# A gated dilated convolution: another hand-written order of all instructions, with seven PSUM evictions moved from ScalarE to VectorE

## The chip, the cores and the metric

The kernel runs on one core of a Trainium2 chip. The metric is the device time of one execution in microseconds (us); the median of three executions stands for a kernel. The core has five engines that each work through a list of their own in order: TensorE (PE, the matmuls, with its weight loads as PEld), VectorE (DVE), ScalarE (ACT), GpSimd (POOL) and SyncE (SP, which here only issues DMAs). They wait for each other by semaphores. DMAs are issued from the queues of SP, ACT and POOL.

## The reference

```python
B, T, D, K = (2, 16000, 256, 3)          # x [B,T,D], w [K,D,2D], w_o [D,D], all bfloat16
dil = 2; pad = (K - 1) * dil
xp = jnp.pad(x, ((0, 0), (pad, 0), (0, 0)))
h = jnp.einsum('btc,cd->btd', xp[:, pad:pad + T, :], w[0])
for i in range(1, K):
    off = pad - i * dil
    h = h + jnp.einsum('btc,cd->btd', xp[:, off:off + T, :], w[i])
z = jnp.tanh(h[..., :D]) * jax.nn.sigmoid(h[..., D:])
return z @ w_o
```

Each output row is a three-tap causal convolution over time with a step of two, split into a tanh half and a sigmoid half, multiplied together, and multiplied by a 256x256 matrix.

## The kernel before

The 32,000 rows are cut into 23 groups. Group 0 (kind P, 640 rows) is computed directly with three taps. The others use the fewer products of a polynomial (Toom-Cook) form of the convolution: 18 groups of kind A (1536 rows: 256 columns of 6 neighbouring rows) need five products for three row pairs, 4 groups of kind B (1024 or 640 rows) four products for two row pairs. A group has four **blocks**, one for each 128 of the 512 output channels, so there are 88 blocks; they run in the order 9, 10, 11, 1 to 8, 12 to 22 of the groups. A product is a pair of matmuls over the 256 input channels with 512 moving columns (320 in the last group, 22).

What a block of kind A does, by the letters of the order: `F` first product into PSUM tile `b`; `c` ScalarE copies `b` to `ss` (L390); `M` middle product added to `b`; `h` VectorE makes `hh` from `ss` and `b` (L393), or `k` ScalarE copies `b` to `hh` (L403); `L` last product added to `b`; `A` VectorE makes `a` in PSUM from `ss` and `b`, `Y` VectorE makes `yy` (both L393); `Z` a product added to `b`, which therefore has to wait until `A` and `Y` have read it; `I` a product added to `a`. Then ScalarE applies tanh or sigmoid to `b`, `yy` and `a` (letters `b`, `y`, `a`, L441), and after two blocks VectorE multiplies tanh by sigmoid (`g`, L460, tile `zz`). `P` is an output product (four matmuls of 256 columns, L478, tile `o_ps`), 123 of them besides the last three. Its result is evicted to SBUF by ScalarE (`e`, L495) or by VectorE (`v`, L487), and `s` stores it.

The moving operands (`u0` to `u3`, `e`, `f`, `uh`, `ud` and for kind B `m`, `p`, `d0`, `d3`) are sums and differences of rows, made by VectorE in one piece (L330, scaled copies L328) or by GpSimd in four quarters (a token with `q`, L330). The sums `rm`, `rp`, `r0`, `ri` are made on top of `e`, `f`, `u0`, `u2`: mostly by an adding DMA from GpSimd's queue (a token that ends in `d`, L325). `rm` is used by `M`, `rp` by `L`, `r0` by `Z`, `ri` by `I`. A quarter on GpSimd is held behind a VectorE instruction so many places back (the number after `q`).

The order of everything is one table, `PLAN`: 1730 tokens, read from left to right; each token appends one piece of work to its engine's list. Nothing else orders the work of the main part. PSUM holds three `b` tiles, two `a` tiles and three `o_ps` tiles.

```python
if "q" in token:   on_gpsimd(token)
elif token[-1] == "d":  pre(*group_of(token[:-1]), None)
else:  note(pre(*group_of(token), nc.vector))
...
elif what in "AY":  combine(next(kinds[what]), what.lower())
elif what in "ev":  out_evict(*pieces[int(token[1:])], on_v=what == "v")
```

Of the kernel before, what the change touches and what calls it, by code (L numbers as in the profile page):

```python
# [26 lines left out]
M ud.1 wa.15q28 b I Y k1 F f.1 a Z f.2 c I b L g x M a A F k2 u2.2 P u1.3q14 c L Y e9 M u1.3q54 A y I k3 rp.1d u3.2
P Y a Z L g e10 Z b A f.3q36 P y ud.2 F f.3q28 b Y P c r0.1d rm.1 P y Z ri.1d e.2 e11 F e.3 I b rm.2d M g c F k4 M
u0.2 u0.3q1 a L h5 c I y A f.3q12 L a M f.3q62 Y e12 P A u1.3q8 e13 Z I Y k6 u1.3q43 I b g ri.2d L a rp.2d F u3.3 y
Z A rm.3d c P u1.4 b r0.2d P a Y M rp.3d F y uh.3 Z ud.3 k7 v15 I b L u3.4 e14 ud.4 F f.4q68 c A P c M u0.3q20 Y a M  # L30
e.4 k8 Z k9 g L rm.4d b I u0.3q33 A e17 P a v16 F f.4q36 L y Y s8 P f.4q55 c x A Z y u2.4q74 M Y b I e18 h10 Z a F g
b P c L u2.3 F e19 u1.5 ri.3d M c A I u0.3q60 k11 M Y a L u0.4 y f.4q1 P A k12 I Z e20 r0.3d uh.4 Y P a rp.4d L b
f.5 r0.4d Z y A F b I g c P u2.5q72 y F Y M e21 u3.5 u2.5q4 I c v22 P y u2.4q90 h13 Z a u2.4q16 v23 M b L u2.4q50
h14 a s10 P s9 e24 u2.5q44 A F x y L Y e.5q82 P c A e.5q79 Z e25 Y M e.5q58 y I h15 b e.5q69 Z a g ri.4d F e26 L c I
A f.6q22 b P s11 uh.5 M a u2.5q82 Y F y rp.5d u0.5 P k16 Z e.6 e27 r0.5d L b g I c P u2.6q118 A y F M e28 u1.6q63 Y
P c f.6q1 h17 Z y I ud.5 e29 rm.5 M b s12 L h18 a u2.6q1 x F a P u2.6q45 A c L Y u1.6q20 e30 I A u1.6q108 e31 M Z a
Y u1.6q33 P k19 g ri.5d Z b L e32 u0.6 P f.7q89 y A I b F uh.6 u2.6q46 e33 P Y c F r0.6d u3.6 P y g rm.6d M e34 I
f.6q13 a h20 P c Z y u1.7 L f.6q67 b M A e35 P rp.6d Y F k21 s14 P a e.7 s13 Z c ud.6 I g e36 ri.6d L b M u2.7q71 A
e37 P a h22 F u0.7q137 e38 P Y u0.7q65 c L s15 Z y uh.7 x u2.7q72 A M b I f.7q90 h23 e39 F f.7q1 y Y L c f.7q114 I
v40 a Z u2.7q22 Y a M g P b P k24 A F e41 x L rp.7 e42 P c A Z y u1.8 I u0.8q93 b M Y a P u0.7q161 h25 Z y F uh.8 b  # L40
u3.7 I u2.8 s16 c rm.7d F e43 f.8 M c L g rp.8d k26 M a u2.7q76 A L k27 Y I y u0.8q1 A Z a u0.7q103 P v44 b u0.8q81
L Y y s17 P u0.8q162 A e45 F r0.7d e46 Z ud.7 Y c I ri.7d P b u3.8 r0.8d M u1.9 a Z e.8 k28 F b ud.8 L rm.8d e.9 c I
y g F u2.9q179 M y A P c P e47 h29 f.9q46 M a Y s18 f.9q43 L e48 s1 ri.8 u2.9q60 Z x k30 I A b L u2.9q117 Y a F y
u0.9q14 A Z c I g u0.9q1 b P a M Y F y u0.9q167 h31 I e49 ud.9 Z c u3.9 L b e.10 rm.9d M e50 A P u0.9q89 a F s19 h32
e51 I x Y f.9q75 c P g L a f.9q1 Z e52 Y P b M u0.10q72 A e53 F u1.10 Z c I h33 y P uh.9 b M f.10 s20 r0.9d y L h34
u2.9q136 F e54 A P a L c Y u0.10q111 I y Y u0.10q129 M e55 Z A rp.9d k35 P uh.10 ri.9d b Z g a I L e56 ud.10 u3.10 F
b s21 A P a x F u2.10 c P Y c M y u1.11 Z e57 M h36 b I u3.11 e58 L g u2.11q137 k37 F P a A L y Y u2.11q107 P c A
u2.11q42 Z y I f.11 rm.10d y M Y b u0.10q118 P e59 v60 rp.10d Z k38 s22 F uh.11 r0.10d b g P a L u0.11 c F P e61 A I
e62 ud.11 ri.10q1 M c Y P y r0.11d u1.12 Z y rp.11d M h39 b I e.11 e63 L u3.12 a F ri.10q1 h40 P e64 A P c ri.10q52
L e65 Y u2.11q33 M a s24 g ri.10q10 Z k41 x I b A L a F u2.12q103 Y y I u2.12q220 A c Z uh.12 rm.11d P y Y P b g M y  # L50
s23 F k42 v66 I u1.13q121 c Z v67 a ri.11d L f.12 e68 M b P A s25 e.13q152 P k43 x Y F a e.13q125 L c e.12 u1.13q170
Z e69 A I b M f.13 u1.13q1 e70 P Y a F u2.12q52 P v71 k44 Z c rp.12d g L y rm.12d M b A I k45 ud.12 P u2.13q69 Y a
s26 F e72 u0.12 L u2.13q15 c Z A P y u2.13q63 M Y b I u1.13q210 e73 h46 F a u2.12q15 Z c uh.13 rp.13d I g y L ri.12d
b M ud.13 P A k47 e.14q113 F a Y L c e.13q247 I A y Z e.14q191 e74 M Y e.13q189 P b h48 Z r0.12d y u3.13 F a g L
rm.13d b I f.14 c P u2.14q103 y F A e75 M v76 u0.13q202 I c h49 P u0.13q57 e77 M Y a u2.14q55 s28 L e78 h50 x
# [591 lines left out]
```

## Time and profile before

| | |
|---|---|
| time, median of 3 runs (lowest, highest) | 258.87 us (258.47, 259.78) |
| time of the profiled execution | 258.77 us |
| its span, first to last instruction | 256.6 us |
| GpSimd busy (share of the span) | 176.9 us (69%) |
| adding DMAs from GpSimd's queue: 18 + 16 + 15 + 15, median from issue to landing | 4.6 to 4.8 us |
| evictions on ScalarE / on VectorE (128x512) | 101 / 23 |

The span is what the instructions cover; about 2.2 us of the profiled execution lie around it. An instruction's time in the trace reaches from its start to its last write, and the next one on the engine may start before that: what an engine can do in a stretch is read from one start to the next, not from the durations.

### The profile page before, as it was taken

The page shows a single profiled execution, that of the slowest core. Times are in us where ns is not written, and L with a number is a line of the kernel's source. Part 1 is how long each engine was busy: PE and PEld are TensorE (multiplying, and loading weights), DVE is VectorE, ACT ScalarE, POOL GpSimd, SP SyncE. Part 2 cuts the span into 40 slices and gives each one's busy share as a digit, 9 for nine tenths or more (in the row PEclk, how much of TensorE's full clock was granted, in tenths as well). Part 3 has the DMA queues.
Part 4 walks back from the last instruction along what each step waited for, and adds up shares of the span by engine and source line. Part 5 has one row for each costly group of instructions (what it writes and reads, how often), then busy time and mean ns, then how long its engine had stood idle before and what let it go on. Part 6 is the DMA issues. An engine that isn't in the chain of part 4 may idle for free.

```text
span 256.6 us, 4575 instructions
## 1 busy us (share of the span) xinstructions
PE 249.9 (97%) x1428; PEld 138.0 (54%) x1428; DVE 242.8 (95%) x405; ACT 243.7 (95%) x492; POOL 176.9 (69%) x249
## 2 busy tenths in 40 slices
PE   8999999999999999999999999999999999999992
PEld 4655555555555565545555555555555545555581
DVE  2999999999999999999999999999999999999991
ACT  4988999999999999999999999999999999999893
POOL 1064554997699888499764887999798798897000
PEclk9999999999999999999999999999999999999997
DMA  6999979989989899999999999996999998773054
GB/s 184 213 202 213 196 172 159 232 143 203 187 199 271 187 200 249 182 289 200 200 237 212 249 196 188 290 244 147 212 260 171 216 219 224 198 217 102 0 226 176
DMA packets 84320, 51.73 MB, mean 202 GB/s; under 512 B 69032, under 2 KB 70312, under 8 KB 84296
## 3 DMA queue, kind: packets, MB, share of 16 engines
q1 hardware_dynamic: 74168, 33.71, 54.3%
q0 software_dynamic: 9216, 16.78, 37.7%
q10 hardware_dynamic: 912, 0.95, 1.1%
q8 instruction: 11, 0.18, 0.3%
q14 instruction: 13, 0.11, 0.1%
HBM read 1.25 MB, written 16.38 MB: 69 GB/s over the span
## 4 chain that ended last, share of the span: by engine, by line
PE 82%; DVE 8%; DMA 3%; ACT 2%; issue 2%; ACTq 0%; DVEq 0%
PE b L359 48%; PE o_ps L478 18%; PE a L359 13%; DVE a L393 2%; DMA e<-u 2%; DVE zz L460 2%; DVE yy L393 2%; PE b L379 1%; PE a L379 1%; DMA xn<-in_x_dram 1%; DVE hh L393 1%; ACT osb L495 1%; ACT sg L441 1%; ACT th L441 0%; ACT ss L390 0%
## 5 line engine op out<-in xcount | busy, mean ns | idle before, releaser
L330 POOL TENSOR_TENSOR u<-xt 128x256 bf16<-128x256 bf16 x88 | 66.8, 774 | 15.0 <-PE b L359 8.4
L478 PE MATMUL o_ps<-wo_sb,zz 128*128 128x256 bf16 x496 | 72.0, 273 | 0.0
L495 ACT CAST osb<-o_ps 128x512 bf16<-128x512 f32 x101 | 63.8, 646 | 0.9 <-PE o_ps L478 0.7
L478 PEld LDWEIGHTS <-zz 128*128 128x128 bf16 x496 | 48.5, 98 | 27.6
L393 DVE SCALAR_TENSOR_TENSOR a<-ss,b 128x512 f32<-128x512 f32 (+1 forms) x88 | 59.5, 679 | 2.3 <-PE b L359 1.3
L390 ACT COPY ss<-b 128x512 f32<-128x512 f32 (+1 forms) x88 | 55.0, 628 | 0.9 <-PE b L359 0.6
L359 PEld LDWEIGHTS <-w_sb 128*128 128x128 bf16 x352 | 34.1, 97 | 35.1 <-issue 3.0
L359 PE MATMUL b<-e,wm_sb 128*128 128x512 bf16 x144 | 42.8, 379 | 0.3 <-DMA e<-u 0.3
L359 PE MATMUL b<-u,w_sb 128*128 128x512 bf16 x144 | 42.9, 379 | 0.2
L359 PE MATMUL b<-u,wa_sb 128*128 128x512 bf16 x144 | 42.9, 379 | 0.0
L359 PE MATMUL b<-f,wp_sb 128*128 128x512 bf16 x144 | 42.9, 379 | 0.0
L359 PE MATMUL a<-u,w_sb 128*128 128x512 bf16 x144 | 42.5, 379 | 0.3 <-DVE a L393 0.2
L460 DVE TENSOR_TENSOR zz<-th,sg 128x1536 bf16<-128x1536 bf16 (+2 forms) x46 | 41.3, 897 | 0.2
L441 ACT ACTIVATE th<-b 128x512 bf16<-128x512 f32 (+1 forms) x44 | 28.0, 636 | 1.4 <-ACT ss L390 0.7
L441 ACT ACTIVATE th<-a 128x512 bf16<-128x512 f32 (+1 forms) x44 | 28.6, 649 | 0.3 <-PE a L359 0.2
L441 ACT ACTIVATE sg<-b 128x512 bf16<-128x512 f32 (+1 forms) x44 | 28.0, 635 | 0.6 <-PE b L359 0.5
L441 ACT ACTIVATE sg<-a 128x512 bf16<-128x512 f32 (+1 forms) x44 | 28.3, 642 | 0.0
L359 PEld LDWEIGHTS <-wm_sb 128*128 128x128 bf16 x176 | 17.0, 98 | 17.2 <-DMA e<-u 1.2
L359 PEld LDWEIGHTS <-wp_sb 128*128 128x128 bf16 x176 | 16.9, 98 | 17.3 <-issue 1.6
L393 DVE SCALAR_TENSOR_TENSOR hh<-ss,b 128x512 f32<-128x512 f32 x38 | 25.9, 681 | 0.2
L393 DVE SCALAR_TENSOR_TENSOR yy<-hh,b 128x512 f32<-128x512 f32 x38 | 25.6, 678 | 0.0
L441 ACT ACTIVATE sg<-yy 128x512 bf16<-128x512 f32 x36 | 24.9, 693 | 0.7 <-DVE yy L393 0.7
(68 smaller groups left out, 373.2 us busy)
## 6 DMA issues: line engine op xcount, KB each, us to landing
out_dram<-osb SPq DMA_DIRECT2D x36, 384.0 KB, 3.5
u<-uh POOLq DMA_DIRECT2D x18, 256.0 KB, 4.8
f<-u POOLq DMA_DIRECT2D x16, 256.0 KB, 4.7
u<-ud POOLq DMA_DIRECT2D x15, 256.0 KB, 4.6
e<-u POOLq DMA_DIRECT2D x15, 256.0 KB, 4.8
out_dram<-osb SPq DMA_DIRECT2D x8, 256.0 KB, 3.1
w_sb<-in_w_dram ACTq DMA_DIRECT2D x3, 256.0 KB, 4.1
xt<-in_x_dram SPq DMA_TRANSPOSE x22, 8.0
```

The lines of the kernel that those rows point to most:

```text
L330: ins = eng.tensor_tensor(out=o, in0=a, in1=b, op=op)
L359: nc.tensor.matmul(G[bank, oi][:, :2 * R], lhsT=wmat[:, ct, osl], rhs=G[mv][:, :, ct, :R], start=which == "first" and ct == 0, stop=ct == ...
L379: nc.tensor.matmul(G[bank, oi][:, :4 * r].rearrange("p (j r) -> p j r", j=4), lhsT=w_taps[tap][:, ct, osl], rhs=xt[:, j0:j0 + 4, ct, c0 + ...
L390: nc.scalar.copy(out=G["ss", oi][:, :n], in_=G["b", oi][:, :n])
L393: return note(nc.vector.scalar_tensor_tensor(out=out, in0=in0, scalar=scalar, in1=in1, op0=ALU.mult, op1=op))
L441: nc.scalar.activation(out=G[name, dt][:, j:j + 2, :R], in_=G[bank, oi][:, :2 * R].rearrange("p (q r) -> p q r", q=2), func=(ACT.Tanh, ACT ...
L460: note(nc.vector.tensor_tensor(out=G["z"][:, dt, :, :n], in0=G["th", dt][:, :, :n], in1=G["sg", dt][:, :, :n], op=ALU.mult))
L478: nc.tensor.matmul(o_ps[:, q, :], lhsT=z, rhs=wo_sb[:, dt, :], start=dt == 0 and (q == 0 or len(dts) == NT), stop=dt == NT - 1, skip_group ...
L495: copy(out=G["osb", at][:, 2 * jp:2 * jp + 2, :], in_=o_ps[:])
```

## The change

`PLAN` is replaced by another list; nothing else in the kernel differs. Both have 1730 tokens and the same blocks, products and loads. By kinds the lists differ in these counts: `e` 103 to 96 and `v` 23 to 30 (seven evictions from ScalarE to VectorE); `h` 38 to 37 and `k` 34 to 35; operands made whole on VectorE, without the scaled ones: 74 in both, of other kinds (`u2` 7 to 13, `rp` 2 to 5, `u0` 10 to 11, `r0` 0 to 1, `d3` 2 to 3, against `u1` 15 to 12, `e` 14 to 11, `f` 11 to 8, `rm` 3 to 0); quarters on GpSimd: 176 in both (`u2` 44 to 20 and `ri` 8 to 0, against `e` 16 to 28, `f` 28 to 40, `u1` 12 to 24, and smaller ones); adding DMAs 64 in both (`rp` 16 to 12, `rm` 15 to 18, `ri` 15 to 17, `r0` 18 to 17).

```diff
 PLAN = """
-m.0 d3.0 p.0 F F d0.0 c F c G L w L A c D wa.5q2 D A wa.2q5 Z d0.1 I b D m.1 a L wa.3q1 F d A wa.10q2 Z c p.1 I
+m.0 d0.0 p.0 F F c G D c D d3.0 L w L A D wa.1q4 F A d wa.2q1 Z c d3.1 I b p.1 Z a I G b F m.1 L c d0.1 P wa.0q1 a L
...
```

The first place is on VectorE at half-way: the rows up to the `yy` of block 44 of the 88 (group 8, last block), the last row but one here. In these rows `a`, `hh` and `yy` are the combinations, `zz` a gate product, `ud` and `u` scaled copies, `e` an operand. Before:

```order
L460 TENSOR_TENSOR zz<-th_1701,sg_1720 128x1536
L393 SCALAR_TENSOR_TENSOR yy<-hh,a 128x512
L393 SCALAR_TENSOR_TENSOR hh<-ss,b 128x512
L328 TENSOR_SCALAR ud<-u_1708 128x1024
L328 TENSOR_SCALAR u_1839<-u_1708 128x1024
L330 TENSOR_TENSOR e<-xt 128x1024
L393 SCALAR_TENSOR_TENSOR a<-ss,b 128x512
L393 SCALAR_TENSOR_TENSOR hh<-ss,b 128x512
L393 SCALAR_TENSOR_TENSOR yy<-hh,b 128x512
L460 TENSOR_TENSOR zz<-th_1787,sg_1811 128x1536
```

Now, with the `yy` of block 44 as the last row:

```order
L460 TENSOR_TENSOR zz<-th_1674,sg_1733 128x1536
L393 SCALAR_TENSOR_TENSOR a<-ss,b 128x512
L393 SCALAR_TENSOR_TENSOR yy<-hh,b 128x512
L328 TENSOR_SCALAR u_1833<-u_1672 128x1024
L330 TENSOR_TENSOR e<-xt 128x1024
L460 TENSOR_TENSOR zz<-th_1774,sg_1789 128x1536
L393 SCALAR_TENSOR_TENSOR a<-ss,b 128x512
L328 TENSOR_SCALAR ud<-u_1672 128x1024
L393 SCALAR_TENSOR_TENSOR yy<-hh,a 128x512
```

The gate product that stood behind this `yy` stands ahead of it now. From the start of the list up to this `yy`, VectorE has one `zz`, one operand, one scaled copy and two evictions more, and one `hh` fewer; TensorE has the same 44 blocks' work ahead of the `Z` that waits for it (211 pairs and 53 output products before, 210 and 54 now).

The second place is on GpSimd at about seven eighths of the list: the quarter of `e` and the adding DMA that makes `rm` (`e<-u`) for group 21, the last of kind A. Before:

```order
L330 TENSOR_TENSOR u_3180<-xt 128x256
L330 TENSOR_TENSOR d_3084<-xt 128x160
L330 TENSOR_TENSOR u_3180<-xt 128x256
L330 TENSOR_TENSOR e<-xt 128x256
L325 DMA e<-u_3151 128x1024
L330 TENSOR_TENSOR u_3224<-xt 128x256
L330 TENSOR_TENSOR p<-xt 128x160
```

Now:

```order
L330 TENSOR_TENSOR e<-xt 128x256
L330 TENSOR_TENSOR d_3101<-xt 128x160
L330 TENSOR_TENSOR e<-xt 128x256 x3
L330 TENSOR_TENSOR d_3222<-xt 128x160
L330 TENSOR_TENSOR f<-xt 128x256
L325 DMA e<-u_3254 128x1024
L325 DMA f<-u_2995 128x1024
```

The four quarters of `e` stand closer together, and two adding DMAs follow each other. Between this DMA's token and the `M` that reads its result (group 21, first block) the list has 12 pairs and 5 output products on TensorE before, and 6 pairs and 3 output products now. For the `rm` of group 19 it is the other way: 8 pairs and 2 output products before, 15 and 4 now.

More of the change, by code (lines that the diff above doesn't have):

```diff
@@ L27 @@
[L27 to L31, printed above, removed]
@@ new lines @@
+c ud.6 I f.7 e35 Z u2.7q9 y A M b P u2.7q89 Y P k21 ri.6d e.7 F a g L rm.7d c Z e36 u2.7q123 A P b M Y y I u2.7q34
+h22 e37 F r0.6d Z a g L c I b A P y ud.7 M Y a F e.8q72 e38 h23 I c Z s15 uh.7 L a rp.7 s14 P x b A f.8q95 M y Y
+e.8q143 F k24 I v39 e.8q130 c Z g y L u0.8q64 b M A P a f.8q27 F k25 Y P e40 ri.7d u0.7 L c Z u1.8 e41 f.8q1 x M A b
+I k26 u3.8 e.8q3 F Y a L c u0.8q139 v42 P y Z u0.8q30 A P y f.8q126 Y I b r0.7d M g e43 F rm.8d k27 Z u2.8 c L s16
+u1.9 b P a f.9 I y F A M e44 P Y c s17 P k28 rp.8 x M y e.9 Z a L h29 e45 I g b L u2.9q72 e46 P A a P uh.8 u2.9q97
@@ new lines @@
+e48 F Y y u0.9q145 v47 Z c u0.8q41 Y y P M b A u2.9q101 I y h30 u2.9q139 Z a uh.9 F b ud.8 L g c ri.8d I e49 F
+u0.9q73 A M c r0.8d Y I k31 M u3.9 a e.10 Z rm.9d k32 L g b P f.10q8 e50 P A L a s19 ud.9 u1.10q165 F y Y x P c
+u0.9q40 A Z y I u1.10q85 Y b M f.10q25 v52 e51 Z u0.9q48 a F h33 P b ri.9d u0.10 L e53 r0.9d g F c P s18 c u1.11q68
+A M e54 I Y y u1.10q9 M h34 a Z u1.10q191 h35 y I u1.11q2 L b L u3.10 u1.11q21 a A F e55 P f.11q51 Y c I f.10q82 Y
+e56 Z a P A u1.11q153 s21 b M s20 rp.9 rm.10d Z y h36 I y F uh.10 b u2.10 L r0.10d c F u3.11 a g M c P k37 Y P
@@ new lines @@
+f.11q1 e57 M A L e58 f.10q28 h38 Z e59 u0.11q27 I A b s22 f.11q27 L x y Y F f.11q144 a Y Z u0.11q47 c P u1.12 b
+u0.11q178 M y A I k39 F rp.11d g Z a L c rp.10 I b f.12q118 A M e60 F ud.10 e.12q61 y Y P c P e.12q96 h40 e61 I
+ri.10d u3.12 a Z e.11 M a g L rm.11d b P k41 e.12q87 Y F e62 P A e63 e.12q21 s23 L c x Z u2.11 u0.11q78 y P A b M
+ud.11 I e64 uh.11 F k42 Y r0.11d P a g Z ri.11d c L b rm.12d u1.13 I e65 M uh.12 e66 ud.12 F e.13q178 A k43 P c
+u2.12 P e.13q213 a L Y M y f.12q31 v68 Z e67 P e.13q194 A b s25 I h44 f.12q24 y s24 F Y y e.13q66 P c L g ri.12d Z
@@ new lines @@
+A F y P h52 e.14q295 c P Y a rm.14d L e83 ud.14 M g y Z I b A P u2.15q55 k53 Y F a P uh.14 c L u3.15 r0.14d g e84 Z
+ri.14d M e85 A I b u2.15q94 P h54 e86 F a Y s31 L c s29 ud.15 P s30 y Y Z x e87 M A b I h55 e.16q193 Z a u1.16
+rp.14q50 I b L y F Y f.16q229 F c A P e.16q84 a M v88 f.16q304 c Z h56 u2.15q129 I b M g rm.15d a F f.15q233 y L h57
+x c P A L y f.16q76 Y M e89 f.16q129 I h58 y f.15q69 P a A Z f.15q27 e90 L Y e.16q18 b I s32 A P e91 u2.15q235 Y Z y
+e.16q273 F b uh.15 I rp.15d g c Z a F u3.16 b M u0.15 P c h59 F a r0.15d M u1.17 e92 ri.15d L c uh.16 P k60 A
@@ new lines @@
+f.17q61 P e93 Y rm.16d M e94 L u0.16 rp.16d k61 I A y Z ud.16 L b u0.17q28 Y P a F g u0.17q44 e95 Z c P A b P
+u0.17q4 v96 M y f.17q5 Y I k62 F g d3.3q36 a Z c L v97 b f.17q57 I A y M r0.16d u2.16 P k63 F Y a ri.16d P c ud.17 L
+u2.17 e98 Z A M ri.17d s35 b P s6 h64 e99 m.3q10 I s33 y Y s34 F e.17q18 a L v101 d3.3q17 Z c A e.17q58 I b Y M
+e.17q6 a P h65 e.17q54 y F g d0.3q59 Z c L e100 I Y f.17q141 b M y A P a F uh.17 u3.17 Z c h66 I rm.17d e102 P g
+rp.17d b L e103 p.3q68 M A a F Y P k67 p.3q112 I c u0.17q60 v105 L y p.3q2 P e104 A r0.17d Z p.3q37 M Y b P h68 a
@@ L72 @@
+m.3q28 Z d3.3q22 y v106 F m.3q21 b L d0.3q66 v107 P m.3q34 c A d3.3q149 F s38 y d0.3q47 s5 M Y c d0.3q250 s36 I h69
+e108 s1 Z s37 y g M s7 a L h70 I b P Y a P A y F g L c Z y A M b I h71 I a Y F a L v109 P e110 Z c v111 y P Y L b P
+A y P A F Z v112 c I b g L a Z I v113 b F P A c s40 F e114 g L s39 I c P a a L A Z e115 A P b v116 Z Z b v117 I s41
+b P g a I P v118 a P e119 g H P v120 s42 R P e121 H e123 v122 H R s44 R e124 s43 e125 s45
 """
```

64 lines of the change are left out of this document (20 added, 44 removed).

## The prediction

> **What bounds the kernel now.** I read the page's first lines first, then its chain of work that ended last, then the groups by form, then rows of the timeline.
>
> ```profile
> span 256.6 us, 4575 instructions
> PE 249.9 (97%) x1428; PEld 138.0 (54%) x1428; DVE 242.8 (95%) x405; ACT 243.7 (95%) x492; POOL 176.9 (69%) x249
> PEclk9999999999999999999999999999999999999997
> PE 82%; DVE 8%; DMA 3%; ACT 2%; issue 2%; ACTq 0%; DVEq 0%
> ```
>
> Three engines are busy for 95% and more, at full clock. The chain runs over TensorE for 82% and, where it leaves it, over VectorE four times as long as over ScalarE (8% against 2%). To see how full each engine really is, one needs the step from start to start. TensorE:
>
> ```profile
> 11.30 1.46 PE L359 MATMUL b<-m,wm_sb 128*128 128x512 bf16 x6
> 12.59 0.60 PE L359 MATMUL b<-p,wp_sb 128*128 128x512 bf16 x2
> ...
> 45.88 1.04 PE L478 MATMUL o_ps<-wo_sb,zz 128*128 128x256 bf16 x8
> 46.75 0.59 PE L359 MATMUL b<-u,w_sb 128*128 128x512 bf16 x2
> ...
> 248.13 0.44 PE L359 MATMUL a<-d,w_sb 128*128 128x320 bf16 x2
> 248.40 0.43 PE L359 MATMUL b<-d,w_sb 128*128 128x320 bf16 x2
> ...
> 250.20 1.47 PE L478 MATMUL o_ps<-wo_sb,zz 128*128 128x256 bf16 x12
> ```
>
> Six matmuls of 512 columns take 1.29 us (0.215 each, 0.43 a pair), eight of 256 take 0.87 (0.109 each, 0.435 an output product), two of 320 take 0.27. The groups by form give the counts:
>
> ```profile
> L359 PE MATMUL b<-u,w_sb 128*128 128x512 bf16 x144 | 42.9, 379 | 0.2
> L359 PE MATMUL b<-d,w_sb 128*128 128x512 bf16 x24 | 7.1, 379 | 0.0
> L478 PE MATMUL o_ps<-wo_sb,zz 128*128 128x256 bf16 x496 | 72.0, 273 | 0.0
> ```
>
> There are five groups of the first form and size (720 matmuls) and four of the second (96), 496 output matmuls and 4 on odd rows, and 38 of 320 columns behind 11.30. That is 816 x 0.215 + 500 x 0.109 + 38 x 0.135 = 235.1 us of work from 11.30 to the end at about 251.5: 240.2 us, so **TensorE loses about 5 us, 2%**. This is all that another order of the same work can win there. VectorE's steps:
>
> ```profile
> 13.29 1.29 DVE L393 SCALAR_TENSOR_TENSOR a<-ss,b 128x512 f32<-128x512 f32 x2 [0.98 <-PE b L359]
> ...
> 51.60 0.69 DVE L393 SCALAR_TENSOR_TENSOR a<-ss,b 128x512 f32<-128x512 f32 x1
> ...
> 63.80 0.68 DVE L393 SCALAR_TENSOR_TENSOR hh<-ss,b 128x512 f32<-128x512 f32 x1
> ...
> 107.54 0.68 DVE L393 SCALAR_TENSOR_TENSOR hh<-ss,b 128x512 f32<-128x512 f32 x1
> 108.14 0.42 DVE L328 TENSOR_SCALAR uh<-u 128x1024 bf16<-128x1024 bf16 x1
> 108.48 0.42 DVE L328 TENSOR_SCALAR u<-u 128x1024 bf16<-128x1024 bf16 x1
> 108.81 0.69 DVE L330 TENSOR_TENSOR u<-xt 128x1024 bf16<-128x1024 bf16 x1
> 109.42 0.69 DVE L330 TENSOR_TENSOR f<-xt 128x1024 bf16<-128x1024 bf16 x1
> 110.02 0.95 DVE L460 TENSOR_TENSOR zz<-th,sg 128x1536 bf16<-128x1536 bf16 x1
> 110.89 0.69 DVE L393 SCALAR_TENSOR_TENSOR a<-ss,b 128x512 f32<-128x512 f32 x1
> 111.49 0.68 DVE L393 SCALAR_TENSOR_TENSOR yy<-hh,b 128x512 f32<-128x512 f32 x1
> 112.09 0.69 DVE L393 SCALAR_TENSOR_TENSOR a<-ss,b 128x512 f32<-128x512 f32 x1
> 112.68 0.69 DVE L487 CAST osb<-o_ps 128x512 bf16<-128x512 f32 x1
> 113.28 0.68 DVE L393 SCALAR_TENSOR_TENSOR yy<-hh,a 128x512 f32<-128x512 f32 x1
> ...
> 117.89 0.96 DVE L460 TENSOR_TENSOR zz<-th,sg 128x1536 bf16<-128x1536 bf16 x1
> ...
> 127.62 0.68 DVE L393 SCALAR_TENSOR_TENSOR yy<-hh,b 128x512 f32<-128x512 f32 x1
> 128.22 1.08 DVE L460 TENSOR_TENSOR zz<-th,sg 128x1536 bf16<-128x1536 bf16 x1
> ```
>
> A scaled copy steps 0.335, an operand 0.605, a gate product `zz` 0.87, a combination `a`, `hh` or `yy` and an eviction 0.598 (four steps in the 2.39 from 110.89 to 113.28). The `yy` of block 44 of 88, half-way, starts at 127.62. The list up to it holds on VectorE 90 combinations (90 x 0.598), 14 large gate products (12.2 us), 6 middle ones (3.6) and the two small ones with their odd rows (1.0), 51 operands (30.9), 29 scaled copies (9.7) and 6 evictions (3.6): 114.8 us. Of it 2.9 lie ahead of 13.29. So VectorE did 111.9 us of work in the 114.9 us from 13.29 to 128.22, and **lost 3.0**. TensorE's side of the same point is the `Z` behind that `yy`:
>
> ```profile
> 128.60 0.38 PE L359 MATMUL b<-u,w_sb 128*128 128x512 bf16 x1
> ```
>
> Ahead of it lie 211 pairs, 53 output products and 3 x 0.27: 114.6 us of work in 117.3 us from 11.30, so 2.7 lost; the other 2.4 are lost behind it. In the first half TensorE and VectorE have the same amount of work and both run nearly full.
>
> **The change, part by part.** *Evictions.* One of 128x512 costs VectorE the 0.60 above; on ScalarE its step is half of the time from the pair below to the next row, 0.475:
>
> ```profile
> 195.73 1.09 ACT L495 CAST osb<-o_ps 128x512 bf16<-128x512 f32 x2
> 196.68 0.63 ACT L390 COPY ss<-b 128x512 f32<-128x512 f32 x1
> ```
>
> Seven on VectorE are +4.2 us, one `hh` less is -0.6, whole operands cancel (74 and 74): VectorE gets **+3.6 us** of work, ScalarE -7 x 0.475 + one copy = -2.9. TensorE's and GpSimd's sums do not change. What counts is where these lie.
>
> *First half.* Up to the `yy` of block 44 VectorE now has one gate product (+0.87), one operand (+0.605), one scaled copy (+0.335) and two evictions (+1.2) more and one `hh` (-0.60) less: **+2.41 us**, with the same TensorE work ahead of the waiting `Z`. ScalarE's list there loses three evictions and gains one `hh` copy and a few activations by their places: about -0.4, which is little relief. Without any loss VectorE would be through at 13.29 + 111.9 + 2.4 = 127.6, 0.6 earlier than the 128.22 of before; with the loss of before, 3.0, it would be 2.4 later. These are the two ends. The loss of before is partly made of waits for a TensorE that was itself full, and more work in VectorE's queue fills these. Its rows show both: from 107.54 to 117.89 lie 19 instructions of 10.36 us in 10.35 us, so no loss; from 51.60 to 63.80 lie 21 instructions of 11.8 us in 12.2 us, so 0.4, or 3%. I take half of the old loss, 1.5 us, between these rows: the `Z` of block 44 starts **0.9 us later**.
>
> *Second half.* At the `yy` of block 72 (group 18, last) VectorE's list is 3.27 us longer than before (three evictions, two `hh`, one operand more, one scaled copy less), but 2.16 us of TensorE work more (four pairs, one output product) stand ahead of that `Z`. Its lead over the old list has shrunk from 2.4 to 1.1: between blocks 44 and 72 VectorE has 1.3 us less to do for the same TensorE work. Of the 2.4 us that TensorE loses in this half, this can give back 0 to 1.3; I take **0.5 earlier**, nearer to the lower end, since part of the loss is a DMA's. Behind block 72 VectorE is no longer full, and the 1.2 us that the new list has more there beside the same work are hidden by the gaps that these rows show (0.56 and 1.46 idle); were these gone, it would be up to 1.2 later:
>
> ```profile
> 228.00:240.00 12.00, 12.00 (x69) 6.49 (x68) 11.44 (x18) 11.32 (x24) 7.51 (x12) 1.00 0.28 83
> 240.00:252.00 12.00, 11.67 (x91) 8.67 (x89) 10.54 (x20) 10.80 (x26) 0.00 (x0) 1.00 0.40 154
> ```
>
> *Adding DMAs.* The one that TensorE visibly waited for is `rm` of group 19:
>
> ```profile
> 206.81 0.61 PE L359 MATMUL b<-e,wm_sb 128*128 128x512 bf16 x2 [0.34 <-DMA e<-u]
> ```
>
> ```profile
> e<-u POOLq DMA_DIRECT2D x15, 256.0 KB, 4.8
> ```
>
> That token had 8 x 0.43 + 2 x 0.435 = 4.3 us of TensorE work between it and its `M`, against 4.8 to land; now 15 pairs and 4 products, 8.2 us, so the wait goes: -0.3. But `rm` of group 21 has 6 x 0.43 + 3 x 0.435 = 3.9 us now (7.3 before), under the 4.8: from 0, if GpSimd is ahead of its token, to +0.9. I take +0.3, by the row of the shorter lead before, and the two cancel. Start and tail keep their work: four operands ahead of the first `a` as before, and at the end the same last gate, output products and store: 0.
>
> *Sum*: +0.9 - 0.5 + 0 = +0.4. The profiled execution of before took 258.77 (span 256.6 and 2.2 around it), 0.1 below the median of 258.87: **259.2 us**.
>
> **The rivals.** *VectorE's queue decides* (slower). If its losses are as large as before, because they come from the round over `b` (TensorE, ScalarE's copy, VectorE, TensorE) and not from spare time, the 2.4 us stay at block 44, and nothing comes back behind it: 258.77 + 2.4 = 261.2. It decides as soon as the loss in the first half is over 1.9 us, 1.7% of it. For it speaks VectorE's 8% of the chain and the 51.60 row's stretch; against it the full stretch at 107.54. The Trainium skill, Perfetto Trace Analysis, section Optimizing Scalar/DVE Operations, has a rule against this change: a saturated VectorE is to hand work to ScalarE, and it puts the fixed access cost of an instruction on PSUM at about 125 ns for VectorE and 51 for ScalarE. By that cost alone I estimate an eviction at 0.475 + 0.074 = 0.55 on VectorE and +3.2 us for the change; the rows say 0.60 and +3.6, and agree on the side.
>
> *The order fits better* (faster). If VectorE loses no more than in its full stretch, block 44 comes 0.6 earlier, the second half gives back its 1.3, and the waits for DMAs cost nothing (-0.3): 258.77 - 2.2 = 256.6; with half of that, 257.7. Against it: the least possible for TensorE is 5 us away only if no wait is left at all, and VectorE's bound at block 44 then has no spare.
>
> *The late `rm`* (slower by up to 0.9, or 1.4 if it lands as late as the 5.33 us of the DMA below): 259.2 + 0.6 = 259.8, or 260.3. It needs GpSimd to run no earlier than its token.
>
> ```profile
> 201.43 5.33 DMA e<-u
> ```
>
> *The list moves no time*: ScalarE and VectorE change, TensorE is full anyway: 258.8. It lies within my forecast's own range.
>
> **How the numbers follow.** Forecast, with the list that moves no time: 0.52. VectorE decides: 0.20; the late `rm` over 0.5%: 0.06; the order fits better: 0.22. A measurement of this kernel can tell about 0.5% (1.3 us) from no change: within it lie 257.6 to 260.2, the likeliest case's own range. So faster 0.22, same 0.52, slower 0.26. For 8 in 10 the range reaches to the rivals, 261.2 above and 257.2, between the two prices of the faster case, below.
>
> **What would show it.** VectorE's busy time near 246.5 and ScalarE's near 241, with 30 and 94 evictions. The 32nd `yy` (block 44) at 128.5, its `Z` at 129.5; at 131 the slower rival is right, below 128.3 the faster one. The `e<-u` wait gone from group 19; one of group 21 at about 230. VectorE's share of the chain at or over 8%. I am wrong if the loss in the second half grows, since I let VectorE give back time there, or if the chain moves to ScalarE or GpSimd.

## The result and the profile after

| | before | changed |
|---|---|---|
| time, median | 258.67 us (4 runs, 258.31 to 259.78) | 262.5 us (4 runs) |
| ratio, 95% interval | 1 | 1.0122 (1.0085 to 1.0159) |
| profiled execution, span | 258.77, 256.6 us | 262.5, 260.2 us |

The changed kernel is slower by 1.2%, 3.2 us by the ratio; the forecast was +0.4 and its range ended at 261.2. Some executions of a kernel are disturbed and longer by up to 7%; the ratios here and below leave them out, so that a median can stand higher than its ratio says.

The page of the changed kernel, its lines on the engines, the chain and the adding DMAs:

```profile
span 260.2 us, 4563 instructions
PE 250.5 (96%) x1428; PEld 137.9 (53%) x1428; DVE 246.2 (95%) x411; ACT 243.0 (93%) x486; POOL 177.9 (68%) x249
...
PE 49%; DVE 22%; ACT 11%; DMA 8%; issue 6%; POOL 2%; ACTq 0%; DVEq 0%
...
e<-u POOLq DMA_DIRECT2D x18, 256.0 KB, 5.0
...
u<-ud POOLq DMA_DIRECT2D x17, 256.0 KB, 5.1
```

VectorE's busy time, 246.2, is where it was forecast (246.5), but that is luck: stretched instructions count as busy, and the same list without the stretch in its second half was busy for 243.7 (e14, below). The chain now leaves TensorE half of the time, for VectorE (22%, before 8%), ScalarE (11%, 2%) and DMAs (8%, 3%). Where, the two `Z` of the prediction say first, then the waits. The timeline of TensorE (start, us, engine, line, operation, tiles), at the `Z` of block 44 and at that of block 72:

```profile
130.37 0.59 PE L359 MATMUL b<-u,w_sb 128*128 128x512 bf16 x2
...
213.28 0.59 PE L359 MATMUL b<-u,w_sb 128*128 128x512 bf16 x2
```

And the second of these points in the kernel before:

```profile
207.69 0.60 PE L359 MATMUL b<-u,w_sb 128*128 128x512 bf16 x2
```

At block 44 the changed order is 130.37 - 128.60 = 1.8 us late (forecast 0.9). At block 72 it is 213.28 - 207.69 - 2.16 (the work that it has done more of by then) = 3.4 late, where 0.4 was forecast, and at the end 3.7. So half of the loss comes in each half, and the second half, which was to give time back, takes 1.7. TensorE's waits in the changed kernel, by the same view (in brackets the idle time and what ended it):

```profile
70.75 0.61 PE L359 MATMUL b<-f,wp_sb 128*128 128x512 bf16 x2 [1.08 <-DMA f<-u]
...
99.74 0.59 PE L359 MATMUL a<-u,w_sb 128*128 128x512 bf16 x2 [0.74 <-DMA u<-ud]
...
167.40 0.60 PE L359 MATMUL b<-u,w_sb 128*128 128x512 bf16 x2 [0.42 <-DVE yy L393]
175.25 0.60 PE L478 MATMUL o_ps<-wo_sb,zz 128*128 128x256 bf16 x4 [0.32 <-DVE osb L487]
176.44 0.60 PE L359 MATMUL b<-f,wp_sb 128*128 128x512 bf16 x2 [0.17 <-DVE hh L393]
179.92 0.59 PE L359 MATMUL b<-f,wp_sb 128*128 128x512 bf16 x2 [0.27 <-DVE hh L393]
181.11 0.59 PE L359 MATMUL b<-u,w_sb 128*128 128x512 bf16 x2 [0.17 <-DVE yy L393]
189.79 0.59 PE L359 MATMUL b<-f,wp_sb 128*128 128x512 bf16 x2 [0.29 <-DVE hh L393]
```

Two waits for adding DMAs in the first half, 1.8 us, and six for VectorE between 166 and 190, 1.6 us by the brackets (2.6 by the steps from start to start). None stands at group 21, where I had feared a late `rm`, and the one of group 19 is gone.

**The two DMAs.** The chain of waits has both, and SP's timeline has a load of `x` beside each:

```profile
62.77 7.93 DMA f<-u
...
90.38 9.32 DMA u<-ud
```

```profile
60.38 7.18 SPq L167 DMA_TRANSPOSE xt<-in_x_dram  x1
...
85.19 7.27 SPq L167 DMA_TRANSPOSE xt<-in_x_dram  x1
```

They took 7.9 and 9.3 us to land, against a median of 5. (The second number of a load's row is the time that SP spent on issuing it; these two loads landed 11.5 and 11.8 us after their issue.) The view of the DMAs between 63 and 68 us (busy share of the 16 DMA engines in 40 slices, packets of each queue, issues with their time to landing; adding DMAs are `q0`, loads and stores `q1`) shows what they waited for:

```profile
DMA  4999999999999900000000000000010000199999
...
DMA packets 2192, 0.58 MB, mean 115 GB/s; under 512 B 2190, under 2 KB 2190, under 8 KB 2191
...
q1 hardware_dynamic: 2191, 0.56, 119.1%
...
f<-u POOLq DMA_DIRECT2D x1, 256.0 KB, 7.9
u<-ud POOLq DMA_DIRECT2D x1, 256.0 KB, 8.7
```

In these 5 us two adding DMAs had been issued (62.77 and 63.36), and not one packet of theirs moved, though the engines stand at 0 for half of the window; their first comes at 68.94 us, where the load's stream of packets ends.

**VectorE between 164 and 184.** Its timeline:

```profile
165.00 1.16 DVE L330 TENSOR_TENSOR u<-xt 128x1024 bf16<-128x1024 bf16 x1
...
169.18 1.29 DVE L460 TENSOR_TENSOR zz<-th,sg 128x1536 bf16<-128x1536 bf16 x1
...
172.28 0.93 DVE L330 TENSOR_TENSOR u<-xt 128x1024 bf16<-128x1024 bf16 x1
...
173.72 0.87 DVE L328 TENSOR_SCALAR u<-u 128x1024 bf16<-128x1024 bf16 x1
...
178.11 1.16 DVE L330 TENSOR_TENSOR f<-xt 128x1024 bf16<-128x1024 bf16 x1
...
182.85 1.49 DVE L460 TENSOR_TENSOR zz<-th,sg 128x1536 bf16<-128x1536 bf16 x1
```

GpSimd's, beside it:

```profile
164.22 1.38 POOL L330 TENSOR_TENSOR e<-xt 128x256 bf16<-128x256 bf16 x1
...
168.99 0.67 POOL L330 TENSOR_TENSOR u<-xt 128x256 bf16<-128x256 bf16 x1
...
171.99 1.74 POOL L330 TENSOR_TENSOR e<-xt 128x256 bf16<-128x256 bf16 x2 [0.64 <-PE b L359]
173.69 1.43 POOL L330 TENSOR_TENSOR u<-xt 128x256 bf16<-128x256 bf16 x2
...
178.00 1.75 POOL L330 TENSOR_TENSOR u<-xt 128x256 bf16<-128x256 bf16 x2 [1.17 <-PE a L359]
...
182.23 1.29 POOL L330 TENSOR_TENSOR f<-f,u 128x256 bf16<-128x256 bf16 x2
```

An operand takes 0.69 us elsewhere, a gate product 0.95, a scaled copy 0.42 (rows of the prediction). These six instructions, all of which read SBUF alone, took 2.5 us more than that together, each while GpSimd made a quarter; the combinations and evictions, which read PSUM, kept their 0.68. Between 144 and 192 us all such rows together are stretched by 3.1 us in the changed kernel and by only 0.6 in the one before; its longer ones lie behind 200, where VectorE has gaps. The Trainium skill, SBUF — State Buffer, section Who interferes with whom, gives the reason: VectorE's second port is GpSimd's only one, and whoever holds it shuts the other out. The trace agrees.

Not every overlap costs VectorE time. Between 13 and 250 us of the changed kernel, 53 of its instructions on SBUF alone overlap a quarter. Of the 34 that started ahead of the quarter, one is stretched by over 0.1 us; of the 19 that started while a quarter ran, ten are; of the 104 that overlap none, none is. In the kernel before it is 1 of 34 and 11 of 26. Why the changed order has more of the costly kind in this stretch isn't shown.

### The profile page after: what moved, and what is told of

Same layout as the page of the kernel before. It is cut to its first block, busy times and chain, and to the rows that moved or that the text cites. A ratio compares the mean times of both kernels' runs of the same rounds, so it can differ in the third digit from the quotient of the medians.

```text
span 260.2 us, 4563 instructions
## 1 busy us (share of the span) xinstructions
PE 250.5 (96%) x1428; PEld 137.9 (53%) x1428; DVE 246.2 (95%) x411; ACT 243.0 (93%) x486; POOL 177.9 (68%) x249
## 4 chain that ended last, share of the span: by engine, by line
PE 49%; DVE 22%; ACT 11%; DMA 8%; issue 6%; POOL 2%; ACTq 0%; DVEq 0%
PE b L359 29%; PE o_ps L478 10%; PE a L359 8%; DVE a L393 5%; ACT sg L441 4%; DMA u<-ud 4%; DVE yy L393 4%; DMA f<-u 3%; DVE zz L460 3%; ACT th L441 3%; DVE u L330 3%; ACT osb L495 2%; DVE hh L393 2%; ACT ss L390 2%; PE b L379 1%
## 5 line engine op out<-in xcount | busy, mean ns | idle before, releaser
L330 POOL TENSOR_TENSOR u<-xt 128x256 bf16<-128x256 bf16 x72 | 54.5, 768 | 15.8 <-PE a L359 6.5
L495 ACT CAST osb<-o_ps 128x512 bf16<-128x512 f32 x94 | 58.9, 649 | 1.2 <-PE o_ps L478 1.1
L390 ACT COPY ss<-b 128x512 f32<-128x512 f32 (+1 forms) x88 | 54.3, 620 | 1.4 <-PE b L359 0.6
L330 POOL TENSOR_TENSOR f<-xt 128x256 bf16<-128x256 bf16 x40 | 30.5, 768 | 4.2 <-PE b L359 2.9
L441 ACT ACTIVATE th<-a 128x512 bf16<-128x512 f32 (+1 forms) x44 | 28.0, 636 | 0.6 <-PE a L359 0.5
L330 POOL TENSOR_TENSOR e<-xt 128x256 bf16<-128x256 bf16 x28 | 22.8, 821 | 5.8 <-PE b L359 3.4
L330 DVE TENSOR_TENSOR u<-xt 128x1024 bf16<-128x1024 bf16 x36 | 25.3, 715 | 0.0
```

The source lines that it names most:

```text
L330: ins = eng.tensor_tensor(out=o, in0=a, in1=b, op=op)
L390: nc.scalar.copy(out=G["ss", oi][:, :n], in_=G["b", oi][:, :n])
L441: nc.scalar.activation(out=G[name, dt][:, j:j + 2, :R], in_=G[bank, oi][:, :2 * R].rearrange("p (q r) -> p q r", q=2), func=(ACT.Tanh, ACT ...
L495: copy(out=G["osb", at][:, 2 * jp:2 * jp + 2, :], in_=o_ps[:])
```

## The experiments

Two theories stood against the list itself. **D**: the two adding DMAs that met a load. **G**: GpSimd's quarters beside VectorE instructions, in a stretch where VectorE has no spare time. **V**, their rival: the evictions. Every ratio is against runs of the kernel before on the same chip.

| run | edit | median (lowest to highest), us | ratio (95%) |
|---|---|---|---|
| e0_again | changed kernel | 261.37 (260.96 to 262.1) | 1.0104 (1.0089 to 1.0119) |
| e2_evict | evictions back | 261.66 (261.63 to 261.91) | 1.0115 (1.0102 to 1.0128) |
| e1_loads | two loads held | 263.4 (261.74 to 267.24) | 1.0161 (1.0132 to 1.0191) |
| e5_loads2 | one earlier, one held | 266.83 (265.82 to 270.18) | 1.0302 (1.0267 to 1.0337) |
| e9_loads3 | both later | 268.24 (265.97 to 269.17) | 1.0353 (1.0315 to 1.0390) |
| e7_before_loads | before, three held | 262.67 (262.34 to 263.7) | 1.0150 (1.0122 to 1.0179) |
| e3_hold | quarters held | 267.29 (263.76 to 271.43) | 1.0283 (1.0240 to 1.0325) |
| e10_gap | ten quarters moved | 265.62 (261.5 to 268.78) | none |
| e6_zeros | 35 quarters zeros | 262.63 (259.06 to 278.1) | 1.0035 (1.0013 to 1.0058) |
| e12_before_zeros | before, 40 zeros | 258.71 (258.04 to 273.1) | 0.9984 (0.9964 to 1.0004) |
| e8_both | e5 and e6 | 264.16 (263.54 to 264.83) | 1.0202 (1.0174 to 1.0229) |
| e11_both | e9 and e10 | 267.67 (264.01 to 276.13) | 1.0297 (1.0243 to 1.0351) |
| e13_early | DMA earlier | 260.3 (259.92 to 263.56) | 1.0076 (1.0047 to 1.0106) |
| e14_both | e13 and e6 | 259.49 (258.76 to 267.99) | 1.0024 (1.0002 to 1.0045) |

### The changed kernel again (e0_again)

The file is that of the changed kernel.

> The changed kernel once more, as the base of the three below: 260.9 to 262.5 us as in its first runs. If the two long waits of TensorE for adding DMAs (1.24 and 0.90 us in the profile) differ from run to run, its times spread over about 2 us; if they are in every run, the spread is that of the kernel before, under 1 us.

In its profile the two waits for DMAs have shrunk. TensorE's timeline, at the second of them and at the two `Z`:

```profile
98.43 0.59 PE L359 MATMUL a<-u,w_sb 128*128 128x512 bf16 x2 [0.18 <-DMA u<-ud]
...
129.07 0.59 PE L359 MATMUL b<-u,w_sb 128*128 128x512 bf16 x2
...
212.15 0.59 PE L359 MATMUL b<-u,w_sb 128*128 128x512 bf16 x2
```

From start to start both waits came to 0.57 us, against 2.14 in the first profile, and the profiled execution was 1.13 us shorter. Block 44 is 0.5 late here, within the forecast; block 72 is 2.3 late, so that between the two 1.8 us are lost, as in the first profile (1.7). In these two profiles the late DMAs vary, and the loss of the second half doesn't.

### The evictions back on ScalarE (e2_evict)

```diff
-f.10q25 v52 e51 Z u0.9q48
+f.10q25 e52 e51 Z u0.9q47
...
```

The same for `v68`, `v69`, `v73`, `v78`, `v80`, `v88`; the other 72 edits only recount the places of quarters behind which fewer instructions now lie, so that each stays behind the one that it was behind.

> Seven evictions of groups 12 to 16 go back from VectorE to ScalarE (30 to 23, 96 to 103), at their places in the list; all else stays. Theory V: the waits for VectorE between 160 and 195 us (2.6 us) mostly go, 2 us or more less than the changed kernel. Theory D: these waits are not what the seven evictions make, 0 to 0.7 less, and the two waits for adding DMAs stay. Theory G (GpSimd's quarters stretch VectorE's SBUF instructions there): about 1 less, since VectorE gets 4.2 us of room to absorb them.

The time doesn't fall. TensorE's waits in the stretch are now

```profile
162.99 0.59 PE L358 MATMUL b<-u,wa_sb 128*128 128x512 bf16 x2 [0.50 <-ACT th L440]
...
187.05 0.59 PE L358 MATMUL b<-f,wp_sb 128*128 128x512 bf16 x2 [0.34 <-ACT hh L402]
```

(the line numbers are one lower in this file). The two longest waits there are now for ScalarE, which is as full as VectorE. V falls: not where the seven evictions run costs the time. G's expectation of 1 us less missed too: the stretched rows between 144 and 192 us came to 4.2 us (3.1 in the changed kernel), so that the overlap took back part of the room that the evictions left. The rule that the prediction weighed (the Trainium skill, Perfetto Trace Analysis, section Optimizing Scalar/DVE Operations: where VectorE is saturated, handing work to ScalarE may make sense) has nothing to give here.

### The loads moved away from the adding DMAs (e1_loads, e5_loads2, e9_loads3, e7_before_loads)

`x` is the token of a load. `X` is new: a load that also waits for the piece that VectorE made last. e1:

```diff
-k9 F x A
+k9 F A
-Z ri.3d uh.4
+Z ri.3d r0.3d uh.4
-F g P b
+F g X P b
-y M r0.3d e.4
+y M e.4
-u1.6q104 F x e28
+u1.6q104 F e28
-ri.5d Y
+ri.5d X Y
```

> Two transposing loads of x are held back until the adding DMAs of groups 4 and 6 are issued, and one adding DMA (r0 of group 4) is issued earlier; all else stays. Theory D (an adding DMA that is issued while a transposing load moves lands only behind it, and TensorE waits for it): both waits go, 2.1 us less than the changed kernel, the adding DMAs in question land in 3.3 to 5.5 us in place of 7.9 and 9.3. Theory V (VectorE's longer list is what sets the time, and the DMA waits only use up time that would be lost anyway): at most 0.7 less.

The first wait went. The second load was issued 0.45 us behind the adding DMA, which is not far enough: it took 9.82 us to land.

```profile
100.38 0.59 PE L358 MATMUL a<-u,w_sb 128*128 128x512 bf16 x2 [1.20 <-DMA u<-ud]
```

e5 keeps the first half of this and puts the second load ahead of two stores instead:

```diff
-b u1.6q64 s11 P
+b u1.6q64 X s11 P
```

> As e1_loads, but the transposing load for group 12 is issued earlier, ahead of two stores and of the adding DMAs of group 6, in place of 0.45 us behind the last of them; r0 of group 4 is issued earlier as in e1_loads. Theory D: both waits for adding DMAs (0.23 to 1.24 and 0.34 to 1.36 us in the profiles so far) go, 0.6 to 2 us less than the changed kernel (261.4): 259.4 to 260.8; ri of group 6 lands in under 6 us. Rival (the waits only use up time that VectorE and ScalarE would cost anyway): 261.0 or more.

Both waits for adding DMAs are gone, and the time is about 5 us longer than the changed kernel's. SP works its list in order, so the stores stood behind two loads. In the timelines of SP, ScalarE (an eviction waits 3.19 us for a store to give its tile free) and TensorE:

```profile
72.49 15.87 SPq L167 DMA_TRANSPOSE xt<-in_x_dram  x2
...
95.18 1.07 ACT L495 CAST osb<-o_ps 128x512 bf16<-128x512 f32 x2 [3.19 <-DMA out_dram<-osb]
...
97.80 1.01 PE L359 MATMUL b<-e,wm_sb 128*128 128x512 bf16 x2 [2.80 <-ACT ss L390]
```

e9 puts it behind the next stores:

```diff
-k19 s12 Z
+k19 s12 X Z
```

> The changed kernel with two transposing loads held later: that for group 7 as in e1_loads, that for group 12 behind two stores that followed it and some 3 us behind the adding DMA of ri for group 6; r0 of group 4 issued earlier. Stores and operands keep their places otherwise. Theory D: neither wait for an adding DMA is left, no wait of ScalarE for a store arises, 0.6 to 1.5 us less than the changed kernel (261.4). Rival (any moved load meets another DMA or makes GpSimd wait for its rows): 261.4 or more.

Again both waits went, and again new ones came: the load issued at 91.00 took 16.84 us to land, two other adding DMAs behind it (issued at 92.30 and 99.16) took 14.22 and 13.06 in place of some 5, and TensorE waited for them, 1.3 us at 106.6 and 3.2 at 112.4. GpSimd, in order as well, waited 7.97 us for the rows of the late load.

In the kernel before, three adding DMAs that TensorE waited for (0.7 us in sum, the `rm` of group 19 among them) also met a load. e7 holds these loads:

```diff
-L g x M
+L g M
-L h5 c
+L h5 X c
-Z k41 x I
+Z k41 I
...
```

> In the kernel before, three transposing loads (groups 6, 19 and 22) are held back until the adding DMAs that landed just in time there (rp of group 2, rm of group 15, rm of group 19) are issued. Theory D: their waits (0.11, 0.07 and 0.51 us of TensorE) go, 0.3 to 0.7 less than before: 258.2 to 258.5. Rival: the held loads run into other adding DMAs, and nothing or more is lost: 258.8 or more.

The three waits are gone, so the meeting was their cause in the old order too. But GpSimd waited for the rows of group 22, and the adding DMAs queued behind that came late:

```profile
223.34 1.03 PE L359 MATMUL b<-f,wp_sb 128*128 128x512 bf16 x2 [2.62 <-DMA f<-u]
224.16 1.06 PE L478 MATMUL o_ps<-wo_sb,zz 128*128 128x256 bf16 x4
225.02 1.06 PE L359 MATMUL b<-u,w_sb 128*128 128x512 bf16 x2
...
226.99 0.60 PE L359 MATMUL b<-e,wm_sb 128*128 128x512 bf16 x2
```

These four show what removes the waits, not what they cost: in each, a moved load made a worse one, and all missed the gain expected of theory D. e13, below, was made for that.

### GpSimd's quarters (e3_hold, e10_gap, e6_zeros, e12_before_zeros)

Where the expectations say blocks 52 to 68, these are, by their first products, blocks 57 to 70. e3 holds 33 of the 35 quarters there behind later VectorE instructions, those that read PSUM:

```diff
-e.13q178 A k43 P c u2.12 P e.13q213
+e.13q0 A k43 P c u2.12 P e.13q0
...
```

> 33 of the 35 quarters on GpSimd between blocks 52 and 68 are held behind the VectorE instruction just ahead of one that reads PSUM; all else stays. Theory G: the stretched VectorE instructions between 144 and 192 us (3.1 us above their usual durations) fall below 1 us, and the time falls by 1.5 to 2. Theories D and V: no less time, or some more, since GpSimd's operands come later.

Inconclusive: the stretch fell (3.1 to 1.9 us, not below 1), but the operands came late, and TensorE waited 1.5 us at 180.8 and 2.5 at 187.2 for the adding DMAs behind them. e10 moves only ten:

```diff
-e.12q21 s23
+s23
-Z u2.11 u0.11q78 y
+Z u2.11 e.12q0 u0.11q0 y
...
```

> The changed kernel with ten quarters on GpSimd, those that ran beside a stretched VectorE instruction between 153 and 184 us, moved or held just behind that instruction; nothing left out. Theory G: the seven stretched instructions (together 3.0 us over their usual durations) fall to under 1 us, TensorE's waits between 160 and 190 us (2.8 us) halve at least, 1.3 us or more less than the changed kernel. Rival: the overlap moves on to the next SBUF instructions, and the time stays within 0.7.

A miss: the overlap moved on to other VectorE instructions (2.8 us of stretch, 3.1 in the changed kernel), and the two lowest executions, 261.5 and 261.78, lie where those of e0_again do. GpSimd is busy for 41 of the 48 us there, which leaves a moved quarter little room. e6 takes the quarters' reads away:

```diff
-ins = eng.tensor_tensor(out=o, in0=a, in1=b, op=op)
+ins = eng.memset(o, 0.0) if zero else eng.tensor_tensor(out=o, in0=a, in1=b, op=op)
```

with `z` behind the 35 tokens between `ri.11d` and `rm.15d`. The result lacks the sums of these quarters; the run tells only what they cost.

> In the changed kernel the 35 quarters that GpSimd makes between blocks 52 and 68 are written as zeros, so that GpSimd reads no operands there: 35 of its 176 quarters are left out of the computation. Theory G (GpSimd's quarters stretch VectorE's SBUF instructions, and TensorE waits behind them): the stretched VectorE instructions between 144 and 192 us (3.1 to 3.3 us over their usual durations) fall under 0.5 us, TensorE's waits between 160 and 190 us (2.8 us) mostly go, 2 us or more less than the changed kernel. Theory V' (VectorE's and ScalarE's lists are too full there by themselves): the stretch goes, the waits stay, under 1 us less.

From 1.0104 to 1.0035: 1.8 us, a little under the 2 expected. The same between the same marks in the kernel before:

> The kernel before with the 40 quarters that GpSimd makes between the same two marks of its list (ri of group 15, rm of group 19) written as zeros, as in e6_zeros; 40 of 176 quarters are left out of the computation. Theory G says that before these quarters cost little, since only two VectorE instructions are stretched there (0.9 us together): 0 to 0.7 less than before in undisturbed runs. If it gains 2 us as the changed kernel did (261.4 to about 259.3), the overlap is not what tells the two orders apart.

There it gains 0.4 us (0.9984; the interval reaches from a gain of 0.9 to none). The overlap is removed from the same part of both orders, and the new one had paid more for it in its time. A memset is also shorter than the sum that it replaces (0.31 against 0.62 us), so that GpSimd was through sooner. That this is the cause instead isn't ruled out by these two runs alone; against it, the waits at 166 to 190 are for VectorE, not for GpSimd or its DMAs, and VectorE was hardly ever idle there (the windows below). The section of the Trainium skill named above says that VectorE's two-input instructions clash with a GpSimd instruction that reads SBUF, and not with one that only writes it; this pair of runs agrees.

### Both together (e8_both, e11_both), and the one that moves the DMA (e13_early, e14_both)

e8 is e5 with the zeros of e6, e11 is e9 with the moves of e10.

> The edits of e5_loads2 and e6_zeros together (35 of 176 quarters are zeros and left out). If the waits for adding DMAs and the stretched VectorE instructions are all that the changed order lost, the sum of both gains: 256.5 to 258.5, at or below the kernel before. If they only stand for the tightness of the list, 259.5 or more.

> The edits of e9_loads3 and e10_gap together, nothing left out. If these two are what the changed order lost: 258.0 to 259.5, as the kernel before. If not: 260 or more.

e8 gains 2.6 us on e5 by its ratio, and no wait of TensorE's over 0.2 us is left between 130 and 230; the store's wait of e5 stays (3.04 us at 98.09). e11 shows no gain on e9 that its interval could tell. Both missed what was expected of the two causes together, since each carries the new wait of its moved load. e13 leaves the second load where it is and issues the adding DMA some 8 us earlier, ahead of it (the first load and its adding DMA as in e1):

```diff
-u2.5 k16 Z
+u2.5 k16 ri.5d Z
-e32 F ri.5d Y
+e32 F Y
```

> The changed kernel with the two adding DMAs that met a transposing load kept apart from it, this time without moving the load that stands between stores: the load of group 7 goes behind the two adding DMAs it met (as in an earlier run, where that wait vanished), and the adding DMA of ri of group 6 is issued some 7 us earlier, ahead of the load at 84.5. Nothing else differs. Theory D (an adding DMA issued while a transposing load moves lands 4 us late, and the two waits for it are a loss of their own): the TensorE waits for an adding DMA at 70 and 99 us are gone, no other wait of over 0.6 us appears ahead of 110, and the time is 0.3 to 2 us below the changed kernel's: 260.0 to 261.2, by how much of these waits the changed kernel has in the same executions. Rival (the time lost there is slack that other waits take up at once): 261.4 or more, with TensorE's waits in sum as in the changed kernel (7.7 to 9.0 us).

Nine of twelve executions lie between 259.92 and 260.99. The profiled one, 263.3, is one of the three others. In it both waits are gone; but ahead of the edited places another adding DMA, the first `rm`, met a load and took 10.31 us instead of 4.5 (e0_again):

```profile
37.35 0.60 PE L359 MATMUL b<-e,wm_sb 128*128 128x512 bf16 x2 [1.65 <-DMA e<-u]
```

By the medians, D's two waits cost 1.1 us (261.37 to 260.3), by the ratios 0.7. The intervals of the ratios overlap, so the times alone point to a price without proving it; what the profiles show is that the waits come with the meeting and go without it.

> The kernel of the run above, and besides the 35 operand quarters that GpSimd makes beside blocks 57 to 70 are written as zeros (left out: these quarters' sums). If the waits for late adding DMAs and the overlap of GpSimd's quarters with VectorE are together the loss of the changed order: 258.0 to 259.0, the level of the kernel before (258.7; 258.3 with its quarters as zeros), and no TensorE wait of over 0.4 us between 60 and 190. If a third cause is needed: 259.5 or more.

It gave 1.0024, 0.6 us over the kernel before, and 258.76 in its profile: between the two numbers expected. No wait of over 0.4 us is left between 60 and 190. Its timeline of TensorE, at the two `Z`:

```profile
129.32 0.59 PE L359 MATMUL b<-u,w_sb 128*128 128x512 bf16 x2
...
209.84 0.60 PE L359 MATMUL b<-u,w_sb 128*128 128x512 bf16 x2
```

And that of e12, the kernel before with zeros:

```profile
128.69 0.59 PE L359 MATMUL b<-u,w_sb 128*128 128x512 bf16 x2
...
207.30 0.59 PE L359 MATMUL b<-u,w_sb 128*128 128x512 bf16 x2
```

Between them the new order is 0.6 late at block 44, 209.84 - 207.30 - 2.16 = 0.4 at block 72, and 258.76 - 258.25 = 0.5 at the end; by the ratios 1.0. With the two causes out, the lists stand about as the prediction had them (0.9, 0.4, 0.4). The busy times between 144 and 192 us, of before, changed and e14 in this order (window, its length, PE, PEld, DVE, ACT and POOL busy with their instructions), close it:

```profile
144.00:192.00 48.00, 48.00 (x272) 26.18 (x270) 47.73 (x80) 47.96 (x99) 41.67 (x56) 1.00 1.04 221
```

```profile
144.00:192.00 48.00, 46.33 (x262) 25.19 (x261) 47.83 (x76) 46.30 (x93) 41.03 (x54) 1.00 1.05 205
```

```profile
144.00:192.00 48.00, 47.90 (x276) 26.60 (x275) 47.83 (x81) 47.77 (x98) 29.46 (x56) 1.00 1.08 207
```

VectorE is busy for all of the window in each. In the changed kernel it got through 76 instructions in it, in e14 through 81, and TensorE, which waits for it, lost 1.67 us in the one and 0.10 in the other. A busy share can't tell work from being shut out.

No version here beats the kernel before: the best without zeros, e13, is 0.8% behind it.

## Why the prediction was wrong, step by step

- *First half, +0.9*: right for the lists. VectorE lost about 1.5 us up to block 44 in e0_again, as I had assumed (128.97 where the next instruction starts, less 13.12 for the first `a`, 111.9 and 2.41); block 44 was 0.5 late there, and 0.6 with both causes taken out. In the first profile it was 1.8 late, and the difference is the two late DMAs.
- *Adding DMAs, "the two cancel"*: failed. The wait of group 19 went as said, that of group 21 didn't come. But I chose the two places by their leads against a median landing of 4.8 us, and landing isn't one number: beside a load it is 7 to 10. Twenty of the 64 took over 6 us in the changed kernel, nine in the one before. What had to be compared was where each order puts them against the loads on SP. The missing term was +0.7 us by the ratios (e13, not clear of noise) and +1.2 by the lateness of block 44 in the first profile.
- *Second half, -0.5*: the step that failed most. "VectorE has 1.3 us less to do for the same TensorE work" holds for the list, and with the quarters' reads gone the half gave 0.2 back (0.6 to 0.4). But every duration of an instruction on SBUF alone that I summed came from rows without a GpSimd read beside them; the one row that I showed beside a quarter, the `zz` at 128.22 with 1.08 us in place of 0.95, I passed over. In this stretch the stretched rows of both orders differ by 2.5 us (3.1 against 0.6), more than the 1.3 that VectorE had to spare; the half took 1.7 to 1.8. The missing term was 1.3 (e14) to 1.8 us (e6), of which about 0.4 (e12; 0 to 0.9 by its interval) is in the order of before too.
- *VectorE's work, +3.6 and 246.5 busy*: the counts hold, and the busy time was met by luck. With the quarters' reads gone it is 243.7 in the new order and 241.9 in the old (e14, e12), +1.8, so that a sum of steps doesn't give the busy time.
- *Start and tail, 0*: right within 0.3 us (block 72 2.3 late, the end 2.6, in e0_again).
- *ScalarE near 241*: 243.0. The evictions' own sum fell from 63.8 to 58.9 us, but ScalarE's instructions overlap each other less where they don't queue, so that its busy time fell by only 0.7. The time doesn't hang on this.
- *VectorE's chain share at or over 8%*: 22%. I named a growing loss in the second half as what would prove me wrong, and it did.
- *The slower rival*, 261.2, came nearest by its number and not by its mechanism: it put 2.4 us at block 44, from the round over `b`, and needed a loss of over 1.9 us there. e0_again, with little of the late DMAs, shows about 1.5 and a block 44 that is 0.5 late.

By ratios, of the 2.7 us that e0_again is slower, 0.7 goes with the DMAs kept apart from loads (e13), 1.3 more with the quarters' reads (e14), of which about 0.4 is in the order of before as well, and 0.6 to 1.0 is left for the lists themselves. Each of these parts is uncertain by half a microsecond or so. Whether the overlap in this order can be avoided with all sums made, I couldn't show: both tries at it failed.

## What to carry to other kernels

Where an order is changed and all engines are full, sum the durations for what runs beside them: list which GpSimd reads will still run when a VectorE instruction that reads only SBUF starts, and whether VectorE has spare time there. For each just-in-time DMA, look for the load it will meet, rather than compare its lead with a median landing; and try first to move the small DMA, not the load: three of the tries with a moved load made what stands behind them (stores, other adding DMAs, GpSimd's list) wait for longer than the wait that was removed.

## What the runs showed of the hardware

While a transposing load moves, an adding DMA issued behind it gets nothing through: no packet of `q0` in the 5 us shown, with the DMA engines partly idle. Over the whole of the changed kernel, cut into half microseconds, 135 slices hold over 200 packets of a load; five of these hold more than 20 packets of adding DMAs, where the slices in which adding DMAs move without a load hold 41 on average. The Trainium skill, DMA: Bandwidth & Descriptors, section Queues, rings and completion order, has each engine take turns between its queues, a packet at a time; these rows do not look like that, and why isn't shown.

After some waits of 2.5 us and more TensorE ran at half speed. The granted clock was 0.50 in e7 from 222.97 to 226.36 and in e5 from 96.98 to 103.79, and 1.00 around these. In e7's rows a pair steps 0.82 to 0.86 us from 223.34 on, instead of 0.43; the five pairs and products up to 226.99 take 3.65 us, 1.5 more than at full speed, and behind that it is back. No wait of up to 1.7 us was followed by it, and two of about 3 us, in e3 and e9, weren't either. The Trainium skill, TensorE: Matmul & The Clock Gate, section What's actually happening, tells of half a clock after an idle window of about 3.4 us that runs freely, and full clock after a busy one of the same length; the trace agrees with the half and with the length of the slow stretch (3.4 us in e7, twice that in e5), but most of the waits ahead of it, 2.5 to 3.8 us, were shorter than that window, and what decides which of them is followed by it isn't shown. Where it strikes, a long wait is dearer by half or more: in e7 1.5 us of slow matmuls on 2.6 us of waiting.
